# A transformer block on one core: an earlier bound for the third head group, spare banks and matmuls of ones in forced waits, a repeated bias column, and a summed residual in the tail

## The chip, the core and the metric

The kernel runs on one core of a Trainium2 chip. The metric is the device time of one execution in microseconds, lower is better; times are medians of several executions. Before the change the three runs shown took 1149.47, 1150.96 and 1151.28 us, so the median is 1150.96 us. The profile was taken of one further execution of 1149.56 us.

## What is computed

One pre-norm transformer block for 2048 rows of width 1024, in bfloat16, with 32 heads of width 32 and a hidden width of 3584:

```python
def _A_ref(x, wqkv, wo):                      # softmax attention, 32 heads
    qkv = (x @ wqkv) -> q, k, v per head
    p = softmax(q @ k.T * Dh ** -0.5)
    return (p @ v) @ wo
def _B_ref(x, w1, b1, w2, b2):
    return gelu_tanh(x @ w1 + b1) @ w2 + b2

h  = x + _A_ref(_layernorm(x), wqkv, wo)
h2 = h + _B_ref(_layernorm(h), w1, b1, w2, b2)
```

## The kernel before, in words

The kernel is written out by a small planner in Python. Every instruction is recorded as a task with what it reads and writes and with an assumed cost; the planner keeps a clock for each engine, decides from these clocks which instruction comes next on TensorE (PE), and so fixes one order for each engine. The chip then runs each engine's list in that order, with semaphores for the dependences. An assumed cost therefore changes the order, not only a number.

**The exponentials.** Softmax is done in 512 units (`u`, numbered from 0). A unit is one block of queries of 256 rows, one group `g` of four heads and 256 keys. The scores of a unit (`qk`, L1130) fill four PSUM banks (two pairs); ScalarE (ACT) then makes two exponentials of 128x1024 elements (L1139), one for each pair. Units use three pairs of banks, 0/1, 2/3 and 4/5, in turn, two pairs for each unit. Bank 6 (`OD`) gathers the products with the values and the sums (`pv`, L1215); bank 7 alone is left for everything else. Eight units of one head group and one query half make an item; `finish_item` (L1226 to L1230) divides at its end on VectorE (DVE). There are 64 items; each head group of the first 512 queries takes two, so that group 2 (the third) begins at unit 32 and group 5 (the sixth) at unit 80.

**The bound.** An exponential needs a bias, so that it cannot overflow. The bias of a group is made from the largest norm of its keys and of its queries: `sumsq` (four matmuls at L632 and a maximum, L635), then `spread` (a diagonal L643, one matmul L529, a maximum L646), then four small DVE instructions in `bias_of` (L675 to L681). The first exponential of a new group cannot start before.

**Fill.** Between scores and value products the planner places other matmuls, called fill here: a generator yields them one after the other. `fill0` makes the keys (`proj_k`), queries (`proj_q`) and values (`proj_v`) that are not there yet, group by group, with the steps of the bounds (`knorm_a`, `knorm_b`, `qnorm_a`, `qnorm_b`) put beside a named group; then come the feed-forward parts (`ffn`) of each block of 512 rows. A fill group of eight matmuls of 512 columns goes to bank 7 and is read out by DVE (`evac`) before the next can open the bank. A matmul is issued as four matmuls on four quarters of the array side by side (`wide`, L529); four such count as one step in what follows.

**Forced waits.** `qk_prereq` runs ahead of the scores of a unit. Where a mark (a bound, a query block, a flag) is missing, `until` issues fill until it is there. Everything so issued stands on PE ahead of the scores.

**Feed-forward.** In `ffn` the sums with `w1` are read out with the bias and halved in one instruction (`tensor_scalar`, L1538), the rest of the gelu are three DVE instructions and one tanh on ACT (L1550 to L1553) for each pair of column blocks. `rows_out` multiplies with `w2`, adds `b2` (L1448), then the residual (L1451), and stores.

**The tail.** The last block of 512 rows has no exponentials beside it. Its first 256 rows get part of the `w1` product ahead of the end of the exponentials (`early_slices`, slices of 16 steps); the rest runs in `tail` with the gelu on ACT, and `rows_out` at the end, eight times 256 rows by 256 columns.

Of the kernel before, what the change touches and what calls it, by code (L numbers as in the profile page):

```python
# [7 lines left out]
dt = mybir.dt  # L8
# [227 lines left out]
def build_kernel(nc, A_x, A_wqkv, A_wo, B_w1, B_b1, B_w2, B_b2, out):  # L236
# [706 lines left out]
    def fill0():  # L943
        for gen in v_left:
            yield from gen
        load_wkey(2, 0)
        load_wkey(3, 1)

        def key(g, last):
            for tc in range(NCH):  # L950
                if tc == 0 and last is not None:
                    yield from mix(proj_k(g, tc), knorm_a(last))
                elif tc == 1 and last is not None:
                    yield from mix(proj_k(g, tc), knorm_b(last))
                else:
                    yield from proj_k(g, tc)

        yield from key(1, None)
        load_wkey(4, 2)
        load_wqry(4, 3)  # L960
        yield from key(2, 1)
        load_wqry(5, 4)
        load_wqry(6, 5)
        load_wqry(7, 0)
        for tt in range(0, NT, 2):
            yield from proj_v(tt, 1)
        load_wv(1)
        yield from key(3, 2)
        load_wkey(5, 1)
        yield from key(4, 3)  # L970
        load_wkey(6, 2)
        for g in range(4, 8):
            if g < 6:
                yield from mix(proj_q(g, 0), (knorm_a, knorm_b)[g - 4](4))
            else:
                yield from proj_q(g, 0)
        for tt in range(0, NT, 2):
            if tt < 4:
                yield from mix(proj_v(tt, 2), (qnorm_a, qnorm_b)[tt // 2](1, 0))
            else:  # L980
                yield from proj_v(tt, 2)
        yield from key(5, None)
        load_wkey(7, 1)
        yield from key(6, 5)
        for tt in range(0, NT, 2):
            if tt < 4:
                yield from mix(proj_v(tt, 3), (knorm_a, knorm_b)[tt // 2](6))
            else:
                yield from proj_v(tt, 3)
        load_wqry(0, 2)  # L990
        yield from key(7, None)
        load_wqry(1, 1)
        side = deque([knorm_a(7), knorm_b(7)])
        for gq in (1, 0):
            for g in range(gq * 4, gq * 4 + 4):
                if gq == 1 and g in (5, 6):
                    load_wqry(g - 3, g - 2)
                if side:
                    yield from mix(proj_q(g, 1), side.popleft())
                else:  # L1000
                    yield from proj_q(g, 1)
            side = deque([qnorm_a(gq, 1), qnorm_b(gq, 1)])
        while side:
            yield from side.popleft()


    LAST = len(CH) - 1
# [40 lines left out]
        return True  # L1048

    def until(mark, lax=False):  # L1050
        while mark not in marks:
# [27 lines left out]
    def key_of(ci, g):  # L1079
        return ci if ci else NCH + g  # L1080

    def qk_prereq(u):
        ci, g, hf = items[u // NJ]
# [345 lines left out]
    def rows_out(ci, q, t, w2_, gT, B_g, g_ch, ost, B_ost, hch, B_hch, b2s, coming=None):  # L1429
# [6 lines left out]
        for lo_fc, hi_fc, u in ((0, cut, 0), (0, cut, 1), (cut, FC, 0), (cut, FC, 1)):  # L1436
            lo = (t + u) * P
            for fc in range(lo_fc, hi_fc):
                if fc % 8 == 0 and coming:
                    coming.popleft()()  # L1440
                if fc % 2 == 0:
                    yield Need(B_g(fc) + B_g(fc + 1) + [B_w2_[fc // 2]], [B_ps[bank]] if u == 0 and fc == 0 else [],
                               [g_ch[fc + 1]] if fc + 1 in g_ch else [])
                wide(bank, u * 256, 256, gT[:, fc, lo:lo + P], w2[:, fc, :], fc == 0, fc == FC - 1,
                     B_g(fc) + [B_w2_[fc // 2]], [B_ps[bank]] if fc in (0, FC - 1) else [], fc == FC - 1, quad)
        o = (q * 2 + t // 2) % len(B_ost)
        b2_, B_b2_ = b2s
        dve(lambda v: v.tensor_tensor(ost[:, o, :, :], ps[:, bank, :].rearrange("p (u c) -> p u c", u=2),  # L1448
                                      b2_[:, q * 256:(q + 1) * 256].unsqueeze(1).to_broadcast([P, 2, 256]), ALU.add),
            reads=[B_ps[bank]] + B_b2_, writes=[B_ost[o]], cost=690)  # L1450
        add = (E.DVE, lambda v: v.tensor_tensor(ost[:, o, :, :], ost[:, o, :, :], hch[:, t:t + 2, q * 256:(q + 1) * 256], ALU.add),  # L1451
               [B_ost[o]] + [B_hch[2 * (t + u) + q // 2] for u in range(2)], [B_ost[o]], 430)
        r0 = CH[ci][0] + t * P

        def store():
            dma(out2[r0:r0 + 2 * P, q * 256:(q + 1) * 256].rearrange("(u p) c -> p u c", p=P), ost[:, o, :, :], 131072,
                reads=[B_ost[o]], lanes=lanes_o, is_out=True)
            if ci < NCH - 2 and q % 2:
                for u in range(2):
                    load_rows(r0 + 512 + u * P, t + u, q // 2)  # L1460
        stores.append(chain([add, ("call", store, [B_ost[o]], [], 0)]))

    def ffn(ci):
# [62 lines left out]
        for bk in range(FC // 2):  # L1526
            s = w1s[bk]
            for u in range(2):
# [6 lines left out]
                    w2s[0][2].popleft()()  # L1535

                def evac(bank, fc=fc):
                    dve(lambda v: v.tensor_scalar(gT[:, fc, 0:w], ps[:, bank, 0:w], b1f[:, fc:fc + 1], 0.5, ALU.add, ALU.mult),  # L1538
                        reads=[B_ps[bank], Bf_b1f], writes=[B_gT[fc]], cost=100 + 1.2 * w)
                    if fc % 2 == 0:  # L1540
                        return
                    gs = gelu_i[0] % NG
# [69 lines left out]
    def early_slices():  # L1612
# [7 lines left out]
        while early["n"] < FC // 2 - AHEAD and not early["stop"]:  # L1620
# [14 lines left out]
                         [B_ps[bank]] if dc in (0, DC - 1) else [], dc == DC - 1, quad)  # L1635
            for u in range(2):
                fc = 2 * bk + u
                dve(lambda v, fc=fc, u=u: v.tensor_scalar(gT[:, fc, 0:256], ps[:, bank, u * 256:u * 256 + 256], b1f[:, fc:fc + 1], None, ALU.add),
                    reads=[B_ps[bank], Bf_b1f], writes=[B_gT[2 * fc]], cost=420)
        while coming:  # L1640
            coming.popleft()()
# [1 line left out]
    def tail():  # L1643
# [83 lines left out]
            load_more()  # L1727
        while rest:
            rest.popleft()()
        b2s = load_b2(LAST, v_off + 28672)  # L1730
        ost, B_ost = sb("ost_t", [P, 8, 2, 256], dt.bfloat16, nbufs(8), at=f["x3_off"])
        hch, B_hch = last["hch"]
        for q in range(4):
            for t in (0, 2):
                yield from rows_out(LAST, q, t, w2s[q], gT, lambda fc: [B_gT[2 * fc + t // 2]], {}, ost, B_ost, hch, B_hch, b2s)
            if q < 2:
                w2s.append(load_w2(LAST, q + 2, v_off + q * 14336, True))

# [12 lines left out]
    while u < NU or pending:  # L1751
# [63 lines left out]
        elif q_r <= t + 90:  # L1815
            burst()
        else:
            best = min(q_r, p_r if p_r + TURN + step <= due else INF, f_r if f_r + TURN + step <= due else INF)
            if best == INF:
# [131 lines left out]
```

## Time and profile before

| what | value |
|---|---|
| median of three runs | 1150.96 us |
| profiled execution | 1149.56 us, span 1147.8 us |
| PE busy | 1086.5 us (95%) |
| ACT busy | 1042.0 us (91%) |
| DVE busy | 683.3 us (60%) |
| first exponential begins | 52.26 us |
| mean granted PE clock | 0.996 of full |

The span runs from the first instruction to the last; 1.8 us of the execution lie around it. Busy shares are means over stages with different limits, and so it is the idle time of the engine that bounds a stage, and who ended it, that is to be read.

### The profile page before, as it was taken

To read this page: it belongs to the slowest core of one execution; us is meant where nothing else is said; L and a number is where in the kernel's file an instruction comes from. 1 tells how busy PE (TensorE), PEld (TensorE's weight loads), DVE (VectorE), ACT (ScalarE), POOL (GpSimd) and SP (SyncE) were. 2 spreads that over 40 slices of the span, in tenths; PEclk is the share of its full clock that TensorE was granted. 3 is DMA by queue.
4 is the path that set the end of the run, shared out by engine and by line. 5 is a ranking of instruction groups with operands and counts; after the bars stand their busy time and mean duration, and the time that the engine had idled before them with its cause. 6 is when DMAs were issued, how large, how long until landed. Compare 5 with 4: busy or idle time off the path is not lost.

```text
span 1147.8 us, 54608 instructions
## 1 busy us (share of the span) xinstructions
PE 1086.5 (95%) x25370; PEld 658.6 (57%) x25370; DVE 683.3 (60%) x1219; ACT 1042.0 (91%) x1158; POOL 21.2 (2%) x59
## 2 busy tenths in 40 slices
PE   6999999899998999999999999999999999999998
PEld 3646456464444445767444446675544476676887
DVE  8564565555666778545567787545678755556011
ACT  7798999899999999999999999999999999996410
POOL 2100000000000000000000000000000000000000
PEclk9999999999999999999999999999999999999999
DMA  9201000003341244342613343321223332426923
GB/s 264 58 21 40 15 9 3 21 4 103 67 85 58 76 117 115 92 122 60 135 30 95 90 126 99 96 82 31 77 77 109 107 110 72 83 81 187 246 79 87
DMA packets 197941, 98.43 MB, mean 86 GB/s; under 512 B 53328, under 2 KB 194640, under 8 KB 197712
## 3 DMA queue, kind: packets, MB, share of 16 engines
q1 hardware_dynamic: 197712, 94.93, 30.9%
q8 instruction: 198, 3.24, 1.2%
q14 instruction: 31, 0.25, 0.1%
HBM read 88.09 MB, written 4.19 MB: 80 GB/s over the span
## 4 chain that ended last, share of the span: by engine, by line
ACT 50%; PE 33%; issue 10%; DVE 6%; DMA 0%; POOL 0%; ACTq 0%; DVEq 0%; POOLq 0%
ACT PT L1139 47%; PE ps L529 13%; PE ps L524 8%; PE ps L1215 5%; PE ps L1130 4%; ACT tm L1552 3%; DVE lnst L481 1%; PE ps L803 1%; DVE Rg L1228 1%; DVE Rg L1226 1%; DVE QT L1230 1%; PE ps L858 1%; DVE rcp L1227 0%; DVE gT L1538 0%; DVE gT L1553 0%
## 5 line engine op out<-in xcount | busy, mean ns | idle before, releaser
L1139 ACT ACTIVATE PT<-ps 128x1024 bf16<-128x1024 f32 x1024 | 952.0, 1145 | 13.4 <-DVE biasm L681 9.7
L1164 DVE TENSOR_TENSOR FS<-PT 128x1024 bf16<-128x1024 bf16 x252 | 172.2, 688 | 146.7 <-ACT PT L1139 119.0
L1215 PE MATMUL ps<-PT,V 128*32 128x256 bf16 x4096 | 224.9, 274 | 11.6 <-ACT PT L1139 6.1
L1130 PE MATMUL ps<-QT,KT 32*128 32x256 bf16 x4096 | 203.9, 273 | 18.1 <-ACT PT L1139 14.5
L529 PE MATMUL ps<-hnT,w 128*32 128x512 bf16 x2688 | 172.6, 381 | 6.1 <-DVE gT L1538 4.5
L529 PE MATMUL ps<-w,gT 128*32 128x256 bf16 x5376 | 172.6, 273 | 0.7 <-issue 0.6
L1130 PEld LDWEIGHTS ps<-QT,KT 32*128 32x128 bf16 x4096 | 61.1, 92 | 168.0 <-ACT PT L1139 157.7
L529 PEld LDWEIGHTS ps<-w,gT 128*32 128x32 bf16 x5376 | 141.1, 97 | 10.5 <-issue 5.6
L1215 PEld LDWEIGHTS ps<-PT,V 128*32 128x32 bf16 x4096 | 106.0, 96 | 62.0 <-ACT PT L1139 16.2
L1215 PE MATMUL ps<-PT,ones 128*32 128x256 bf16 x2080 | 132.3, 274 | 0.0
L529 PEld LDWEIGHTS ps<-hnT,w 128*32 128x32 bf16 x2688 | 61.5, 96 | 75.5 <-issue 28.4
L1538 DVE TENSOR_SCALAR gT<-ps,b1f 128x512 bf16<-128x512 f32 x84 | 63.0, 750 | 46.0 <-PE ps L529 44.4
L1215 PE MATMUL ps<-FS,ones 128*32 128x256 bf16 x1008 | 72.4, 277 | 0.0
L1215 PEld LDWEIGHTS ps<-PT,ones 128*32 128x32 bf16 x2080 | 56.4, 97 | 10.1
L529 PE MATMUL ps<-xnTe,wk 128*32 128x512 bf16 x832 | 56.6, 395 | 4.3 <-DVE kmax L646 2.3
L1553 DVE SCALAR_TENSOR_TENSOR gT<-tm,gT 128x1024 bf16<-128x1024 bf16 x42 | 51.1, 1219 | 1.4 <-ACT tm L1552 1.0
L1551 DVE SCALAR_TENSOR_TENSOR tm<-tm,gT 128x1024 bf16<-128x1024 bf16 x42 | 51.3, 1222 | 0.9
L1552 ACT ACTIVATE tm<-tm 128x1024 bf16<-128x1024 bf16 x42 | 50.1, 1193 | 0.0
L524 PE MATMUL ps<-w,gT_t 128*128 128x256 bf16 x448 | 49.1, 273 | 0.0
L1448 DVE TENSOR_TENSOR ost_t<-ps,b 128x512 bf16<-128x512 f32 x8 | 5.5, 692 | 72.6 <-PE ps L524 72.6
L524 PEld LDWEIGHTS ps<-w,gT_t 128*128 128x128 bf16 x448 | 43.8, 98 | 5.1
L1678 ACT ACTIVATE gT_t<-ps,b1f 128x256 bf16<-128x256 f32 (+1 forms) x36 | 17.2, 518 | 28.5 <-PE ps L524 28.5
(140 smaller groups left out, 931.4 us busy)
## 6 DMA issues: line engine op xcount, KB each, us to landing
w<-in_B_w_dram SPq DMA_DIRECT2D x42, 512.0 KB, 3.8
w<-in_B_w_dram SPq DMA_DIRECT2D x168, 128.0 KB, 3.6
w_t<-in_B_w_dram SPq DMA_DIRECT2D x12, 512.0 KB, 6.7
xr<-in_A_x_dram SPq DMA_DIRECT2D x16, 256.0 KB, 6.9
wk<-in_A_wqkv_dram SPq DMA_DIRECT2D x16, 256.0 KB, 3.2
wq<-in_A_wqkv_dram SPq DMA_DIRECT2D x16, 256.0 KB, 4.7
w_e<-in_B_w_dram SPq DMA_DIRECT2D x32, 128.0 KB, 2.4
w<-in_B_w_dram SPq DMA_DIRECT2D x14, 256.0 KB, 5.5
```

Source lines behind the costliest of these rows:

```text
L481: steps.append((E.DVE, lambda v, c=c: v.bn_stats(lnst[:, s, i, c * 6:(c + 1) * 6], x_ap[:, c * 512:(c + 1) * 512]), [B_x], [B], 690))
L524: pe(lambda p: p.matmul(ps[:, bank, lo:lo + n], lhsT, rhs, start=start, stop=stop), reads=reads, writes=writes, inc=inc, cost=mm(n))
L529: pe(lambda p, r=r: p.matmul(ps[32 * r:32 * r + 32, bank, lo:lo + n], lhsT[:, 32 * r:32 * r + 32], rhs, start=start, stop=stop, tile_posit ...
L1130: pe(lambda p, k=k, kt=kt, r=r, b=b: p.matmul(ps[:, b, k * 256:(k + 1) * 256], KT[32 * r:32 * r + 32, g, kt * P:(kt + 1) * P], QT[32 * r:3 ...
L1139: act(lambda a, safe, i=i, b=b: a.activation(PT[:, o_, 2 * i:2 * i + 2, :], ps[:, b:b + 2, :], ACT.Exp, bias=0.0 if safe else biasm[:, g, ...
L1164: dve(lambda v: v.tensor_tensor(FS[:, f_, :, :], PT[:, o_, :, 0:256], PT[:, o_, :, 256:512], ALU.add), reads=B_PT[o_], writes=[B_FS[f_]], ...
L1215: pe(lambda p, d=d, r=r, lhsT=lhsT, rhs=rhs, n=n: p.matmul(ps[32 * r:32 * r + 32, OD, d * 256:(d + 1) * 256], lhsT, rhs, start=(start and ...
L1538: dve(lambda v: v.tensor_scalar(gT[:, fc, 0:w], ps[:, bank, 0:w], b1f[:, fc:fc + 1], 0.5, ALU.add, ALU.mult), reads=[B_ps[bank], Bf_b1f], ...
L1551: (E.DVE, lambda v: v.scalar_tensor_tensor(t_, t_, GB, x_, ALU.add, ALU.mult), [Bt] + Bx, [Bt], 1220),
L1552: (E.Activation, lambda a: a.activation(t_, t_, ACT.Tanh, scale=GK), [Bt], [Bt], 946),
L1553: (E.DVE, lambda v: v.scalar_tensor_tensor(x_, t_, 1.0, x_, ALU.add, ALU.mult), [Bt] + Bx, Bx, 1220)])
L1678: act(lambda a: a.activation(gT[:, fc, lo:lo + n], ps[:, bank, o:o + n], ACT.Gelu_apprx_tanh, bias=b1f[:, fc:fc + 1], scale=1.0), reads=[B ...
```

## The change

1. `fill0` lists its groups first and puts side steps ahead of a group by number. The steps of the third group's bound, before beside the first two groups of the next keys, now stand ahead of the last of eight value groups. The other side steps keep their places.
2. A forced wait in `qk_prereq` lets fill use two more banks, the pair that the coming unit doesn't take.
3. In a forced wait, and where the planner sees PE and ACT both idle, matmuls of ones are issued into the coming unit's first bank, as long as the planner's idle time is over 330 ns.
4. The read-out of the `w1` sums adds a repeated column of `b1` with `tensor_tensor`; the halving of the gelu is left out there, its constants follow, and it is done in `rows_out` (by 0.5) for all but the last block. The planner's cost of a read-out is 690 instead of 714.
5. In the tail, residual and `b2` are summed once into an f32 tile `hb` (four DVE instructions); `rows_out` then needs one addition for each store. The last 256 rows by 256 columns are done as two parts of 128 rows with a store each.

```diff
-    GC = 8.0 * 0.044715
-    GB = 2.0 / GC
+    GC = 0.044715
+    GB = 1.0 / GC
...
+        keys(2)
+        loads(asked(load_wqry, 5, 4), asked(load_wqry, 6, 5), asked(load_wqry, 7, 0))
+        beside(7, 7, knorm_a(2), knorm_b(2))
+        vals(1)
+        loads(asked(load_wv, 1))
+        keys(3)
...
     def until(mark, lax=False):
+        if lax and mark not in marks and at_u[0] is not None:
+            k = 2 * ((2 * at_u[0] + 2) % 3)
+            fbanks.items = [7, k, k + 1]
+            fbanks.i = 0
+            until_(mark, lax)
+            fbanks.items = [7]
+        else:
+            until_(mark, lax)
...
+            if lax:
+                awake(fill_ready())
             if not do_fill():
                 raise RuntimeError(f"never made: {mark}")
+
+    def awake(t):
+        b = qk_banks(u)[0]
+        while t < INF and max(plan.free[E.PE], plan.ready(E.PE, [], [B_ps[b]])) + 330 < t:
+            for r in range(4):
+                pe(lambda p, r=r: p.matmul(ps[32 * r:32 * r + 32, b, :], ones_pp[:, 0:32], ones_pp[:].unsqueeze(1).to_broadcast([P, 4, P]),
+                                           start=True, stop=True, tile_position=(0, 32 * r), skip_group_check=True),
+                   reads=[B_ones], writes=[B_ps[b]] if r in (0, 3) else [], inc=r == 3, cost=mm(512) if r == 0 else 1, kind="C")
...
+        if ci == LAST:
+            hb, B_hb = b2s
+            if lone is not None:
+                r0, t, o = r0 + lone * P, t + lone, (o + lone) % len(B_ost)
+                dve(lambda v: v.tensor_tensor(ost[:, o, lone, :], ps[:, bank, lone * 256:lone * 256 + 256], hb[:, t, q * 256:(q + 1) * 256], ALU.add),
+                    reads=[B_ps[bank], B_hb[t]], writes=[B_ost[o]], cost=430)
+                dma(out2[r0:r0 + P, q * 256:(q + 1) * 256], ost[:, o, lone, :], 65536, reads=[B_ost[o]], lanes=lanes_o, is_out=True)
+                return
...
-        dve(lambda v: v.tensor_tensor(ost[:, o, :, :], ps[:, bank, :].rearrange("p (u c) -> p u c", u=2),
-                                      b2_[:, q * 256:(q + 1) * 256].unsqueeze(1).to_broadcast([P, 2, 256]), ALU.add),
+        dve(lambda v: v.scalar_tensor_tensor(ost[:, o, :, :], ps[:, bank, :].rearrange("p (u c) -> p u c", u=2), 0.5 if ci < LAST else 1.0,
+                                             b2_[:, q * 256:(q + 1) * 256].unsqueeze(1).to_broadcast([P, 2, 256]), ALU.mult, ALU.add),
             reads=[B_ps[bank]] + B_b2_, writes=[B_ost[o]], cost=690)
...
-                    dve(lambda v: v.tensor_scalar(gT[:, fc, 0:w], ps[:, bank, 0:w], b1f[:, fc:fc + 1], 0.5, ALU.add, ALU.mult),
-                        reads=[B_ps[bank], Bf_b1f], writes=[B_gT[fc]], cost=100 + 1.2 * w)
+                    dve(lambda v: v.tensor_tensor(gT[:, fc, 0:w], ps[:, bank, 0:w], b1f[:, fc:fc + 1].to_broadcast([P, w]), ALU.add),
+                        reads=[B_ps[bank], Bf_b1f], writes=[B_gT[fc]], cost=690)
...
+        hb, B_hb = b2s = sb("hb", [P, 4, D], dt.float32, nbufs(4), at=xl_off)
+        for t4 in range(4):
+            dve(lambda v, t4=t4: v.tensor_tensor(hb[:, t4, :], hch[:, t4, :], b2_[:], ALU.add),
+                reads=B_hch[2 * t4:2 * t4 + 2] + B_b2_, writes=[B_hb[t4]], cost=1220)
```

More of the change, by code (lines that the diff above doesn't have):

```diff
@@ L947, in fill0 @@
         load_wkey(3, 1)
[L949 to L1002, printed above, removed]
@@ L1003, in fill0, with keys, vals, queries @@
-        while side:
-            yield from side.popleft()
+        groups, sides = [], {}
+        def keys(g):
+            groups.extend(proj_k(g, tc) for tc in range(NCH))
+        def vals(q):
+            groups.extend(proj_v(tt, q) for tt in range(0, NT, 2))
+        def queries(lo, hi, tc):
+            groups.extend(proj_q(g, tc) for g in range(lo, hi))
+        def beside(a, b, ga, gb):
+            sides.setdefault(len(groups) + a, []).append(ga)
+            sides.setdefault(len(groups) + b, []).append(gb)
@@ new lines, in fill0 @@
+        keys(3)
+        loads(asked(load_wkey, 5, 1))
+        beside(0, 1, knorm_a(3), knorm_b(3))
+        keys(4)
+        loads(asked(load_wkey, 6, 2))
+        beside(0, 1, knorm_a(4), knorm_b(4))
+        queries(4, 8, 0)
+        beside(0, 1, qnorm_a(1, 0), qnorm_b(1, 0))
+        vals(2)
+        keys(5)
+        loads(asked(load_wkey, 7, 1))
+        beside(0, 1, knorm_a(5), knorm_b(5))
+        keys(6)
+        beside(0, 1, knorm_a(6), knorm_b(6))
+        vals(3)
+        loads(asked(load_wqry, 0, 2))
@@ new lines, in fill0 @@
+        keys(7)
+        loads(asked(load_wqry, 1, 1))
+        beside(0, 1, knorm_a(7), knorm_b(7))
+        queries(4, 5, 1)
+        loads(asked(load_wqry, 2, 3))
+        queries(5, 6, 1)
+        loads(asked(load_wqry, 3, 4))
+        queries(6, 8, 1)
+        beside(0, 1, qnorm_a(1, 1), qnorm_b(1, 1))
+        queries(0, 4, 1)
+        beside(0, 1, qnorm_a(0, 1), qnorm_b(0, 1))
+        for i, gen in enumerate(groups):
+            for side in sides.pop(i, ()):
+                yield from side
+            yield from gen
@@ L1007, in build_kernel @@
+        for i in sorted(sides):
+            for side in sides[i]:
+                yield from side
     LAST = len(CH) - 1
@@ L1441, in rows_out @@
                 if fc % 2 == 0:
[L1442 removed]
+                    yield Need(B_g(fc) + B_g(fc + 1) + [B_w2_[fc // 2]], [B_ps[bank]] if u == (lone or 0) and fc == 0 else [],
                                [g_ch[fc + 1]] if fc + 1 in g_ch else [])
```

33 lines of the change are left out of this document (27 added, 6 removed).

## Prediction

> **What bounds the kernel now.** I read the busy times on the page, then the waits of ACT, then ACT's timeline where it waits, then the stretches.
>
> ```profile
> PE 1086.5 (95%) x25370; PEld 658.6 (57%) x25370; DVE 683.3 (60%) x1219; ACT 1042.0 (91%) x1158; POOL 21.2 (2%) x59
> ```
> ```profile
> ACT gT_t L1678 <- PE ps L524: 28.5, 19, 8.9
> ACT PT L1139 <- DVE biasm L681: 9.7, 2, 4.8
> ACT PT L1139 <- PE ps L1130: 2.8, 4, 1.2
> ```
> ```profile
> 300.00:1046.30 746.30, 717.33 (x18424) 419.06 (x18416) 488.57 (x803) 744.88 (x811) 9.62 (x21) 1.00 0.34 90
> 1046.30:1144.30 98.00, 96.87 (x881) 82.61 (x880) 18.26 (x35) 21.44 (x41) 1.14 (x3) 1.00 0.57 153
> 1144.30:1147.80 3.50, 0.00 (x0) 0.00 (x0) 1.12 (x2) 0.00 (x0) 0.00 (x0) 1.00 0.13 37
> ```
>
> The stretches list, after their length, the busy time of PE, weight loads, DVE, ACT and POOL, then PE's clock. The highest busy share is PE's, but it doesn't set the pace everywhere. From 300 to 1046 us ACT works 744.88 of 746.30 us, while PE has 29 us to spare: the exponentials set the time. From 1046.3 to 1144.3 it is PE (96.87 of 98.00); then come 3.5 us for the last output. So a gain is worth something in three places only: where ACT waits between exponentials (9.7 + 2.8 us in all), in PE's work after the last exponential, and behind the last matmul. The 28.5 us of L1678 belong to the tail, where PE is the bound.
>
> The waits between exponentials sit in two places (start, length, idle before):
>
> ```profile
> 116.19 1.94 ACT L1139 ACTIVATE PT<-ps 128x1024 bf16<-128x1024 f32 x2 [4.84 <-DVE biasm L681]
> 119.34 2.85 ACT L1139 ACTIVATE PT<-ps 128x1024 bf16<-128x1024 f32 x3 [1.21 <-PE ps L1130]
> ```
> ```profile
> 194.84 11.14 ACT L1139 ACTIVATE PT<-ps 128x1024 bf16<-128x1024 f32 x12
> 210.80 1.94 ACT L1139 ACTIVATE PT<-ps 128x1024 bf16<-128x1024 f32 x2 [4.81 <-DVE biasm L681]
> 213.21 7.54 ACT L1139 ACTIVATE PT<-ps 128x1024 bf16<-128x1024 f32 x8 [0.48 <-PE ps L1130]
> ```
>
> They are the starts of the third group (unit 32) and the sixth (unit 80): 4.84 + 1.21 and 4.81 + 0.48, together **11.34 us**. The rest of the 2.8 us is two waits of 0.56 us far apart, which I leave as they are.
>
> **Part 1, the third group's bound.** The instruction orders of the two programs can be compared without a time. In the new one group 2's norm matmuls stand behind the scores of unit 29 and its diagonal behind those of unit 30, and ACT reads the flag ahead of unit 31's exponentials; the bias is some 1.5 units ahead of its use, and the 4.84 + 1.21 us go. What is late next is the sixth group. Its bound keeps its place in the list of fill, but the old wait at unit 32 had pushed PE's fill ahead; now ACT reaches unit 80 with less fill done. In the old order 8 steps of keys stand between the scores of units 79 and 80, in the new one 18, and ten steps of ones.
>
> What the new wait costs is worked out along the order, with durations of the old wait:
>
> ```profile
> 203.29 0.40 PE L1130 MATMUL ps<-QT,KT 32*128 32x256 bf16 x8 [0.22 <-ACT PT L1139]
> 204.90 1.91 PE L529 MATMUL ps<-xnTe,wk 128*32 128x512 bf16 x32 [0.89 <-DVE kn L635]
> 206.63 0.29 PE L1215 MATMUL ps<-PT,V 128*32 128x256 bf16 x4
> 206.74 0.30 PE L1215 MATMUL ps<-PT,ones 128*32 128x256 bf16 x4
> ...
> 208.23 0.24 PE L529 MATMUL ps<-dg,ones_pp 128*32 128x128 bf16 x4 [0.55 <-DVE dg L643]
> 208.40 0.40 PE L1130 MATMUL ps<-QT,KT 32*128 32x256 bf16 x8
> ```
> ```profile
> 204.07 0.69 DVE L635 TENSOR_REDUCE kn<-ps 128x1 f32<-128x512 f32 x1 [0.56 <-PE ps L632]
> 206.86 0.69 DVE L582 CAST KT<-ps 128x512 bf16<-128x512 f32 x1 [2.10 <-PE ps L529]
> 207.59 0.42 DVE L583 TENSOR_TENSOR sqk<-KT 128x512 bf16<-128x512 bf16 x1
> 207.93 0.25 DVE L643 TENSOR_SCALAR dg<-ident,kn 128x128 bf16<-128x128 bf16 x1
> 208.09 0.44 DVE L1226 STREAM_TRANSPOSE Rg<-ps 128x256 f32<-128x256 f32 x1
> 209.63 0.28 DVE L646 TENSOR_REDUCE kmax<-ps 128x1 f32<-128x128 f32 x1
> ```
>
> - The scores of unit 79 start at 203.29; their row says 0.40 us, the next matmul overlaps a little of it, and I take 0.33. Call 203.62 zero. ACT runs dry at 194.84 + 11.14 = 205.98, that is at 2.36.
> - PE then has 2 steps of keys (32 matmuls took 206.63 - 204.90 = 1.73, so 0.22 a step: 0.43), 9 steps of value products (0.11 each: 1.0), then 8 steps of keys whose read-out starts 206.86 - 204.90 = 1.96 after their begin: 3.4.
> - DVE has in its new order: read-out (0.73 to the next start) and square (0.34), the four instructions that finish an item (209.63 - 208.09 = 1.54), the maximum of norms (0.72), one more read-out and square (1.07), the diagonal (0.25 and 0.05 to its matmul), 0.29 more to the next maximum (the diagonal's matmul of 0.24 and a handover of 0.05), and from there to the exponential 210.80 - 209.63 = 1.17. Sum 6.15.
> - So ACT starts at 3.4 + 6.15 = 9.55, and waits 9.55 - 2.36 = **7.2 us** instead of 4.81.
>
> **Part 2, the spare banks.** The two banks lent to fill at unit 80 are 0 and 1, which are among the four that unit 81 takes for its scores. A fill group opened in one of them must be finished and read out first. In the new order 13 steps of keys stand between the scores of units 80 and 81; the first 8 end a borrowed bank's group. Its read-out ends 0.33 + 1.96 + 0.69 = 2.98 us after the scores of unit 80 start, the exponential can follow some 0.55 us behind that (a handover of 0.1 and 119.34 - 118.89 = 0.45 from scores to exponential), and unit 80's exponentials end 1.3 + 1.94 = 3.24 after those scores start (1.17 + 0.29 - 0.17 from scores to exponential, 208.40 - 208.23 = 0.17 being how far they stand behind the diagonal's matmul): a wait of **0.3 us**, between nothing and the 1.21 us of the old first wait.
>
> ```profile
> 118.89 0.40 PE L1130 MATMUL ps<-QT,KT 32*128 32x256 bf16 x8
> ```
>
> One place is new: between the scores of units 116 and 117 PE's order has a value product that reads unit 116's own exponentials. In the old order that stands only at the two forced waits, in the new only here and at unit 80. There the scores of 117 wait until ACT is done: handover about 0.25, two steps of 0.11, 0.45 to the exponential: **0.9 us**.
>
> New waits: 7.2 + 0.3 + 0.9 = 8.4 us against 11.34: a gain of **2.9 us**.
>
> **Part 3, matmuls of ones.** They are ten steps of 512 columns (2.2 us), all between units 79 and 80 and placed where PE waits for DVE's square and diagonal, so they cost nothing unless they end later than DVE: at worst a few 0.22 us. What they could hold off shows here:
>
> ```profile
> 111.88:115.29 3.41, 1.34 (x36) 0.61 (x28) 2.90 (x8) 0.00 (x0) 0.00 (x0) 1.00 0.05 16
> 115.29:118.71 3.42, 3.35 (x32) 1.13 (x32) 0.63 (x5) 1.94 (x2) 0.00 (x0) 0.52 0.02 5
> 207.46:210.87 3.41, 1.70 (x43) 0.70 (x36) 2.94 (x12) 0.07 (x1) 0.00 (x0) 1.00 0.00 0
> 210.87:214.28 3.41, 3.41 (x44) 1.12 (x40) 1.12 (x2) 2.93 (x4) 0.00 (x0) 0.52 0.01 2
> ```
>
> After 3.41 us in which PE was busy 1.34 and 1.70 us, the clock is at half for the next 3.41 us. That made the 1.21 and 0.48 us behind the old waits; in the new wait PE is filled almost throughout, so I put no half clock there. The Trainium skill (TensorE: Matmul & The Clock Gate, "Why this matters for your kernels") asks only that no idle gap exceeds about 3 us; by that neither old wait would have lost its clock, and the ones would be worth nothing. The rows above speak against it: the longest single gap in them was 1.16 us.
>
> **Part 4, repeated column and planner costs.** The form (f32 from PSUM plus a repeated f32 column) isn't in the trace. Nearest:
>
> ```profile
> L1538 DVE TENSOR_SCALAR gT<-ps,b1f 128x512 bf16<-128x512 f32 x84 | 63.0, 750 | 46.0 <-PE ps L529 44.4
> L1448 DVE TENSOR_TENSOR ost_t<-ps,b 128x512 bf16<-128x512 f32 x8 | 5.5, 692 | 72.6 <-PE ps L524 72.6
> L1551 DVE SCALAR_TENSOR_TENSOR tm<-tm,gT 128x1024 bf16<-128x1024 bf16 x42 | 51.3, 1222 | 0.9
> ```
>
> I take L1448's 692 ns (same size, two tensors), at worst 1222. 84 x 58 ns = 4.9 us less DVE work, under a stage that ACT bounds with 744.88 of 746.30: nothing. The halving in `rows_out` is one more operand on 24 instructions of 0.69 us, nothing either.
>
> **Part 5, the tail.** From the last exponential PE has four projections, what is left of an early slice, and the tail's steps. In the new order the left part is 64 matmuls instead of 16, the tail's own `w1` steps are 336 instead of 352.
>
> ```profile
> 1095.20 49.07 PE L524 MATMUL ps<-w,gT_t 128*128 128x256 bf16 x448
> 1101.52 0.69 DVE L1448 TENSOR_TENSOR ost_t<-ps,b 128x512 bf16<-128x512 f32 x1 [37.82 <-PE ps L524]
> 1144.31 0.69 DVE L1448 TENSOR_TENSOR ost_t<-ps,b 128x512 bf16<-128x512 f32 x1 [4.96 <-PE ps L524]
> 1145.04 0.42 DVE L1451 TENSOR_TENSOR ost_t<-ost_t,hch_t 128x512 bf16<-128x512 bf16 x1
> 1145.49 0.37 SPq L290 DMA_DIRECT2D out_dram<-ost_t  x1
> ```
> ```profile
> L1230 DVE TENSOR_TENSOR QT<-ps,Rg 128x256 bf16<-128x256 f32 x64 | 27.2, 424 | 2.2
> ```
> ```profile
> 1082.86 0.67 SPq L289 DMA_DIRECT2D b<-in_B_b_dram  x1
> ...
> 1107.62 1.26 SPq L290 DMA_DIRECT2D w<-in_B_w_dram  x2
> ```
>
> A step is 49.07 / 448 = 0.109 us: 12 more and 16 fewer, **0.4 us** gained. The four sums into `hb` cost 4 x 1.22 = 4.9 us at most and lie in the 37.82 us in which DVE waits for the first output; they need `b2`, whose load is asked for at 1082.86, 18.7 us ahead of it. Without that cover the first read-out alone would be late, and PE has other banks meanwhile. At the end the store was issued 1145.49 - 1144.31 = 1.18 us after the read-out began. Now one addition of 128x256 stands there; that size with two f32 inputs takes 424 ns (L1230), so 1.18 - 0.45 = **0.7 us** is gained. The store halves; I give that nothing. On SP's queue the loads of the third and fourth `w2` parts now stand behind one more store each, about 1 us; the third part, asked for at 1107.62, is needed half way through the 49.07 us, at 1119.7.
>
> **Sum.** 1149.56 - 2.9 - 0.4 - 0.7 = 1145.6 for the profiled execution. That execution is 1.4 us under the median of 1150.96; for the median 1150.96 - 4.0 = **1147.0 us**.
>
> **Rivals.**
> 1. *The time is given back in full at the sixth group.* The same fill must be done before its bound, so the waits might again add up to 11 us (half clock in spite of the ones, one window at half pace costing 1.7 us, and 1.2 us each at units 81 and 117). For it: PE was busy 95%, and the order does move 10 steps there. Against it: the chain above. Only the tail's 1.1 us would remain: 1149.8.
> 2. *The read-out of `w1` sums is slow* with the repeated column, at L1551's 1222 ns instead of 750. The fill there has one bank, so PE waits each time: 84 x 0.47 = 40 us against PE's 29 us to spare from 300 to 1046; it decides from about 0.35 us more on each. It would give 1147 + 11 = 1158, slower. Against it: L1448, same size, 692.
> 3. *The bound isn't earlier in effect*, because something else holds unit 32 back. The waits stay as before: 1149.8.
>
> **How the numbers follow.** Forecast 0.64, rival 1 0.22, rival 2 0.08, rival 3 0.06. About 0.2% (2.3 us) is what a measurement of this kernel can tell from no change, so faster begins under 1148.7. The forecast's own range is 1144.5 to 1149: 1.5 us either way for the waits, 0.5 for the tail, and what medians of three differ. Rivals 1 and 3 lie up to 1150.5; I leave out rival 2. Range 1144.0 to 1150.5. A little of the forecast falls into the same: faster 0.62, same 0.28, slower 0.10.
>
> **What would show it.** ACT should have no wait for the bias near 111 us and one of about 7.2 us near 200; waits of under 1 us behind it and near 270; no half clock at either start; the read-out of `w1` sums at 0.69 us; 1.1 us less between last exponential and end. A wait over 10 us at the sixth group, a read-out over 1.1 us, or new waits beyond 300 us would make the prediction wrong.

## The result and the profile after

The changed kernel takes **1144.88 us** (median of six runs, 1144.68 to 1145.98) against 1150.95 us for the kernel before (six runs, 1149.47 to 1152.45): 6.07 us less, a ratio of 0.995 with an interval of 0.9938 to 0.9963. Forecast were 1147.0 us, 4.0 less. Two further comparisons of the same two kernels, below, gave 4.1 and 4.3 us less; why the first one is larger is part of what follows. The profiled execution took 1145.98 us with a span of 1144.2, that is 3.6 us less than the profiled one of before.

The page's first part, and what ACT waited for (us in total, times, longest; the row of L1726 belongs to the tail, the other two lie between the exponentials):

```profile
PE 1086.8 (95%) x25445; PEld 655.4 (57%) x25450; DVE 681.5 (60%) x1220; ACT 1041.2 (91%) x1159; POOL 21.8 (2%) x59
```
```profile
ACT gT_t L1726 <- PE ps L524: 28.3, 18, 10.2
ACT PT L1172 <- DVE biasm L681: 7.4, 1, 7.4
ACT PT L1172 <- PE ps L1163: 2.9, 7, 0.8
```

The busy shares tell nothing: they stand as before. The waits for the bias do: two of 4.8 us have become one of 7.4. Waits for scores (L1163) have grown from four to seven, with about the same sum: 0.25 us at unit 60, which the old kernel doesn't have, 0.47 and 0.84 behind the long wait, and four beyond 300 us with 1.4 in all, where the old kernel had two with 1.1. ACT's timeline (start, length, how many exponentials, idle before) says where they are:

```profile
53.19 110.58 ACT L1172 ACTIVATE PT<-ps 128x1024 bf16<-128x1024 f32 x120 [0.37 <-issue]
164.02 37.16 ACT L1172 ACTIVATE PT<-ps 128x1024 bf16<-128x1024 f32 x40 [0.25 <-PE ps L1163]
208.59 1.94 ACT L1172 ACTIVATE PT<-ps 128x1024 bf16<-128x1024 f32 x2 [7.42 <-DVE biasm L681]
211.00 66.28 ACT L1172 ACTIVATE PT<-ps 128x1024 bf16<-128x1024 f32 x72 [0.47 <-PE ps L1163]
278.11 22.10 ACT L1172 ACTIVATE PT<-ps 128x1024 bf16<-128x1024 f32 x24 [0.84 <-PE ps L1163]
...
1043.82 1.28 ACT L1889 ACT_TABLE_LOAD   x1
```

The first line is the point of part 1: 120 exponentials without a stop, past unit 32, where the old kernel waited 4.84 us. The three longest waits are at units 80, 81 and 117: 7.42 + 0.47 + 0.84 = 8.73 us against 11.34. The table load after the last exponential begins 990.63 us after the first exponential, before it was 1046.32 - 52.26 = 994.06: 3.4 us less. From there to the span's end it is 1144.2 - 1043.82 = 100.4 us against 101.5: 1.1 us less. The first exponential itself begins 0.9 us later, which is no part of the change: its start lay between 52.0 and 53.6 us in the profiles of this study, of unchanged programs too. 3.4 + 1.1 - 0.9 = 3.6.

The stretches (length, then busy time of PE, weight loads, DVE, ACT, POOL, then PE's clock, DMA's busy share and GB/s), for the long wait, the exponentials after 300 us, and the tail:

```profile
200.90:208.60 7.70, 7.70 (x152) 3.76 (x148) 5.34 (x15) 0.28 (x2) 0.00 (x0) 1.00 0.16 36
300.00:1043.80 743.80, 715.91 (x18384) 415.76 (x18378) 483.11 (x804) 742.39 (x809) 9.91 (x21) 1.00 0.33 90
1043.80:1140.70 96.90, 95.51 (x904) 81.78 (x906) 20.39 (x34) 21.43 (x43) 1.14 (x3) 1.00 0.61 159
```

In the wait ACT is idle and PE is busy all of 7.70 us at full clock: it is a wait for PE's and DVE's chain, not an idle chip. PE's timeline there, with the value products and a short run of keys left out, shows with what it was filled (L1088 are the matmuls of ones):

```profile
198.69 0.40 PE L1163 MATMUL ps<-QT,KT 32*128 32x256 bf16 x8
...
200.45 1.90 PE L529 MATMUL ps<-xnTl,wk 128*32 128x512 bf16 x32
...
202.61 0.82 PE L1088 MATMUL ps<-ones_pp 128*32 128x512 bf16 x12
203.26 0.73 PE L632 MATMUL ps<-sqk,blk 128*32 128x512 bf16 x4
203.61 2.11 PE L529 MATMUL ps<-xnTe,wk 128*32 128x512 bf16 x32
205.34 1.89 PE L1088 MATMUL ps<-ones_pp 128*32 128x512 bf16 x28
207.13 0.24 PE L529 MATMUL ps<-dg,ones_pp 128*32 128x128 bf16 x4
207.30 0.40 PE L1163 MATMUL ps<-QT,KT 32*128 32x256 bf16 x8
```

The group of keys at 203.61 stands in another bank than the norms' sums of L632 ahead of it, for DVE reads those only later, which in one bank would have held the keys back:

```profile
205.00 0.68 DVE L635 TENSOR_REDUCE kn<-ps 128x1 f32<-128x512 f32 x1
```

The read-out of the `w1` sums and DVE in the tail:

```profile
L1586 DVE TENSOR_TENSOR gT<-ps,b1f 128x512 bf16<-128x512 f32 x84 | 58.0, 690 | 48.4 <-PE ps L529 47.9
```
```profile
1086.02 4.63 DVE L1783 TENSOR_TENSOR hb<-hch_t,b 128x1024 f32<-128x1024 bf16 x4 [23.51 <-DMA b<-in_B_b_dram]
1098.88 0.69 DVE L1491 TENSOR_TENSOR ost_t<-ps,hb 128x512 bf16<-128x512 f32 x1 [8.23 <-PE ps L524]
...
1141.67 0.42 DVE L1487 TENSOR_TENSOR ost_t<-ps,hb 128x256 bf16<-128x256 f32 x1 [2.63 <-PE ps L524]
```

The read-out has fallen from 750 to 690 ns. The four sums into `hb` lie in idle time, and 8.23 us of it are left behind them.

### The profile page after: what moved, and what is told of

It reads as the page before. It is cut to its first block, busy times and chain, and to the rows that moved or that the text cites. A ratio compares the mean times of both kernels' runs of the same rounds, so it can differ in the third digit from the quotient of the medians.

```text
span 1144.2 us, 54773 instructions
## 1 busy us (share of the span) xinstructions
PE 1086.8 (95%) x25445; PEld 655.4 (57%) x25450; DVE 681.5 (60%) x1220; ACT 1041.2 (91%) x1159; POOL 21.8 (2%) x59
## 4 chain that ended last, share of the span: by engine, by line
ACT 44%; PE 40%; issue 9%; DVE 5%; DMA 1%; SPq 0%; POOL 0%; ACTq 0%; DVEq 0%; POOLq 0%
ACT PT L1172 41%; PE ps L529 18%; PE ps L524 7%; PE ps L1248 7%; PE ps L1163 5%; ACT tm L1600 2%; DVE lnst L481 1%; PE ps L803 1%; DVE Rg L1259 1%; DMA w_t<-in_B_w_dram 1%; DVE Rg L1261 1%; PE ps L858 1%; DVE QT L1263 1%; DVE FS L1197 0%; DVE gT L1586 0%
## 5 line engine op out<-in xcount | busy, mean ns | idle before, releaser
L1163 PE MATMUL ps<-QT,KT 32*128 32x256 bf16 x4096 | 203.7, 273 | 20.8 <-ACT PT L1172 15.7
L1163 PEld LDWEIGHTS ps<-QT,KT 32*128 32x128 bf16 x4096 | 60.8, 92 | 172.8 <-ACT PT L1172 160.4
L1586 DVE TENSOR_TENSOR gT<-ps,b1f 128x512 bf16<-128x512 f32 x84 | 58.0, 690 | 48.4 <-PE ps L529 47.9
L1726 ACT ACTIVATE gT_t<-ps,b1f 128x256 bf16<-128x256 f32 (+1 forms) x36 | 16.7, 506 | 28.3 <-PE ps L524 28.3
L1248 PEld LDWEIGHTS ps<-FS,ones 128*32 128x32 bf16 x1016 | 26.7, 95 | 23.5 <-issue 19.2
```

The source lines that it names most:

```text
L1163: pe(lambda p, k=k, kt=kt, r=r, b=b: p.matmul(ps[:, b, k * 256:(k + 1) * 256], KT[32 * r:32 * r + 32, g, kt * P:(kt + 1) * P], QT[32 * r:3 ...
L1248: pe(lambda p, d=d, r=r, lhsT=lhsT, rhs=rhs, n=n: p.matmul(ps[32 * r:32 * r + 32, OD, d * 256:(d + 1) * 256], lhsT, rhs, start=(start and ...
L1586: dve(lambda v: v.tensor_tensor(gT[:, fc, 0:w], ps[:, bank, 0:w], b1f[:, fc:fc + 1].to_broadcast([P, w]), ALU.add), reads=[B_ps[bank], Bf_ ...
L1726: act(lambda a: a.activation(gT[:, fc, lo:lo + n], ps[:, bank, o:o + n], ACT.Gelu_apprx_tanh, bias=b1f[:, fc:fc + 1], scale=1.0), reads=[B ...
```

## The experiments

Two things had to be explained: why the time fell by more than 4.0 us, and which part of the change did it. **Theory A**: what comes on top is half clock. The old kernel loses PE's clock behind its waits, in some executions more than its profile shows, and the changed kernel doesn't, since matmuls of ones and lent banks keep PE busy. The rivals are other places: the bound's move, the read-out or the tail are worth more than the sum gave them. The expectations call the first A; the letters after it stand for such other places. The experiments ran in three groups, each beside the kernel before, which took 1149.57 us beside e1 to e4, 1149.22 beside e5 to e8 and 1149.65 beside e9 to e12. "Full clock" means a mean granted clock of 1.000 over the execution.

**e1, the kernel before once more**, with no edit.

> The kernel before, unchanged, for a second profile. The measured gain of 6.1 us is 2.1 us more than the chain of waits and the tail give (4.0). Theory A: the spells of half clock, which begin in aligned stretches of 3.41 us after a stretch in which PE was busy about half of the time or less, fall differently in each execution; in the profile of before they fell cheaply (1.21 and 0.48 us behind the two waits). Then this profile shows the same two waits for the bias of 4.8 us, but another sum of the waits for the scores, up to 2 us more, and times that spread over about 3 us. Theory B: the rest of the gain comes from the many later stretches (read-out, order of the work). Then the waits between exponentials sum to 12.5 us here as in the first profile, and what is left is a longer time from 300 us on.

1149.70 us, ratio 1.0007 (0.9999 to 1.0016). Its profile fell on an execution of 1148.5 us without any half clock. ACT's waits there, then the stretches that answer to the four that the prediction shows (same work, 0.93 us later behind the first wait, 0.40 earlier behind the second):

```profile
117.12 88.47 ACT L1139 ACTIVATE PT<-ps 128x1024 bf16<-128x1024 f32 x96 [4.83 <-DVE biasm L681]
210.40 90.42 ACT L1139 ACTIVATE PT<-ps 128x1024 bf16<-128x1024 f32 x98 [4.81 <-DVE biasm L681]
```
```profile
112.81:116.22 3.41, 1.34 (x36) 0.61 (x28) 2.89 (x8) 0.00 (x0) 0.00 (x0) 1.00 0.06 20
116.22:119.64 3.42, 2.84 (x56) 1.30 (x60) 1.75 (x7) 2.52 (x3) 0.00 (x0) 1.00 0.02 5
207.06:210.47 3.41, 1.71 (x43) 0.69 (x36) 2.94 (x12) 0.07 (x1) 0.00 (x0) 1.00 0.00 0
210.47:213.88 3.41, 2.90 (x60) 1.09 (x56) 1.12 (x2) 3.41 (x4) 0.00 (x0) 1.00 0.01 2
```

PE is as idle as before (busy 1.34 and 1.71 us of 3.41), yet the next stretch has clock 1.00, and the 1.21 and 0.48 us behind the old waits are gone. So half clock is a matter of the single execution, and those 1.69 us are its price at the two waits, as theory A says. Over 83 executions of the old kernel (e1 and those beside the three groups) the time goes with the mean granted clock: 1147.88 us on average at 1.000 (8 of them), 1149.07 at 0.999 (26), 1149.50 at 0.998 (11), 1150.28 at 0.997 (17), 1151.15 at 0.996 (16); over all, 1149.73. The order isn't strict: the five below 0.996 averaged 1150.3, and the eight at 1.000 lay between 1146.2 and 1148.9. If those eight stand for the kernel without half clock, it costs 1.85 us on average, and 3.3 at a clock of 0.996.

**e2, the changed kernel without ones.**

```diff
     def awake(t):
+        return
```

> The changed kernel without the matmuls of ones; the order of all other instructions is the same. Theory A: PE idles 0.65 and 1.5 us inside the long wait at unit 80, a spell of half clock follows in part of the executions, and the steps of keys behind it take up to 1.7 us longer: median 1145.4 to 1146.5 and a wider spread than the changed kernel's 1.3 us. Theory B, and the rule that only an idle gap of about 3 us costs the clock: no spell, median 1144.9 as with the ones.

1145.15 us, ratio 0.9964 (0.9951 to 0.9977), and full clock in all six runs: no slower. The wait, and the stretch in which it lies:

```profile
208.57 1.94 ACT L1173 ACTIVATE PT<-ps 128x1024 bf16<-128x1024 f32 x2 [7.42 <-DVE biasm L681]
```
```profile
200.90:208.60 7.70, 5.68 (x112) 2.67 (x108) 5.34 (x15) 0.28 (x2) 0.00 (x0) 1.00 0.16 36
```

Without the ones PE is busy 5.68 of 7.70 us, and the clock holds all the same. Theory A expected 1145.4 to 1146.5 us and a wider spread, which was too much: in the changed kernel the ones cost nothing and bring nothing that can be told.

**e3, the changed kernel with one bank for fill.**

```diff
-            fbanks.items = [7, k, k + 1]
+            fbanks.items = [7]
```

> The changed kernel with bank 7 alone in forced waits, ones kept. The same 18 steps of keys stand between units 79 and 80, but each group waits for the read-out of the one before it. Theory A: the wait for the bias grows from 7.4 to about 9.2 us (one read-out and its handovers, 1.2, and the norm matmuls behind a read-out, 0.6), the waits at units 81 and 117 (0.47 and 0.84) go, since their orders are not there: about 1145.5. A rival, that the borrowed banks don't matter because DVE's chain sets the wait: 7.4 us and 1144.

1146.74 us, ratio 0.9973 (0.9964 to 0.9983), 1.6 us more than e2 beside it.

```profile
210.18 90.42 ACT L1172 ACTIVATE PT<-ps 128x1024 bf16<-128x1024 f32 x98 [9.45 <-DVE biasm L681]
```

The wait is 9.45 us, and the 0.47 and 0.84 us behind it are gone with the lent banks. 9.45 - 8.73 = 0.7 us is seen in the waits. The planner also made six early slices here instead of seven, and the profile takes 0.4 us longer than e2's from table load to end (100.5 against 100.1). The remaining 0.5 us was not traced; 1145.5 was expected. All twelve runs had full clock: with the ones, a single bank keeps it too.

**e4, the kernel before with the bound's move alone.**

```diff
+            if tt == NT - 2:
+                yield from knorm_a(2)
+                yield from knorm_b(2)
...
-        yield from key(3, 2)
+        yield from key(3, None)
```

> The kernel before with the third group's bound moved and nothing else. Theory A: the first pair of waits (4.84 + 1.21) goes, the one at unit 80 grows to about 9.2 us with one bank, plus 1 to 2 us of half clock behind it without ones: waits of 10 to 11 us against 11.3, so 1149.5 to 1150.5, hardly a gain: the move alone is given back at the sixth group. If the move by itself is what gains, the wait stays near 7.4 and the time is 1147.

1149.19 us, ratio 1.0000 (0.9989 to 1.0011): the move alone gains nothing in the median. ACT and PE:

```profile
209.43 91.34 ACT L1142 ACTIVATE PT<-ps 128x1024 bf16<-128x1024 f32 x99 [9.45 <-DVE biasm L681]
```
```profile
204.63 1.91 PE L529 MATMUL ps<-xnTe,wk 128*32 128x512 bf16 x32 [1.83 <-DVE kn L635]
207.96 0.24 PE L529 MATMUL ps<-dg,ones_pp 128*32 128x128 bf16 x4 [1.42 <-DVE dg L643]
```

The two waits of 4.8 have become one of 9.45: given back. With a single bank PE stands idle for 1.83 us, until DVE has read the norms' sums (kn), and 1.42 us more, and the executions spread from 1146.70 to 1151.83 us: five at clock 0.998 or less took 1149.1 and more, the three at 1.000 took 1146.7 to 1147.2.

**e5, the kernel before with the ones alone** (the function `awake` and its two calls).

> The kernel before with the matmuls of ones alone: five steps of them ahead of unit 32, four ahead of unit 80, no other order changed. In the first runs on this question the kernel before took 1147.8 us where its mean granted clock was 1.000 and 1150.6 where it was 0.996 or 0.997. Theory A (the part of the gain that the prediction lacked is half clock, which comes and goes between executions): granted clock 1.000 in nearly all executions, waits for the bias as before (4.8 and 4.8 us), median 1147 to 1148, 2 us under the kernel before, spread under 2 us. Theory B (ones are worth nothing, the gain comes from the order): as the kernel before, 1149.5 to 1151.

1147.70 us, ratio 0.9986 (0.9977 to 0.9994), with waits of 4.84 and 4.81 us as in the old kernel. The clock was at least 0.998 in all twelve runs. At an unchanged wait, 1.5 us came from nothing but PE being kept busy: theory A, where it says that the old waits lose clock. The least busy 3.41 us at the two waits now have 2.13 us of PE work, before 1.27 and 1.70. But only five of the twelve had full clock, where nearly all were expected, and the profiled one, at 0.999, shows why: from 819.10 us PE was busy 1.80 us of 3.41, where no bound is awaited and no ones are placed, and from 822.51 to 825.92 the clock was 0.51. The old kernel loses clock at this third place too (rows in the last section). In the profiles of the changed kernel and of e2 no stretch of 3.41 us between the exponentials has less than 1.96 us of PE work, so the third place went without the ones. Which part of the change did that wasn't tested.

**e6, the changed kernel once more**, with no edit.

> The changed kernel again, beside the others on one chip: 1144.9, granted clock 1.000 in all executions. Theory A also wants the difference to an execution of before at full clock to be about 3 us, theory B 6.

1145.15 us, ratio 0.9969 (0.9957 to 0.9981): 4.1 us less than before, not 6.1.

**e7, a value product less early at unit 117.** The planner's choice between two kinds of value products was mended for one branch of its loop, so that none reading unit 116's own exponentials stands ahead of the scores of 117.

```diff
-    def pv():
-        e = sums.popleft() if due_sum() or (sums and plan.ready(E.PE, pv_reads(sums[0]), []) <= plan.free[E.PE] + 150) else pending.popleft()
+    def pv(early=False):
+        s_r = plan.ready(E.PE, pv_reads(sums[0]), []) if sums else INF
+        if early and sums and pending and s_r <= plan.ready(E.PE, pv_reads(pending[0]), []):
+            s_r = 0.0
+        e = sums.popleft() if due_sum() or (sums and s_r <= plan.free[E.PE] + 150) else pending.popleft()
...
```

> The changed kernel with the planner's slip at unit 116 mended: where it chose to place a value product because the sums of a folded unit would be ready first, it then placed another product that waits for the unit's own exponentials. The wait of 0.84 us at unit 117 should go and nothing else change up to there: 0.8 us less than the changed kernel on the same chip, about 1144.1. If the wait comes back later, because PE's fill is what limits the first 128 units, the time is the changed kernel's.

1142.99 us, ratio 0.9949 (0.9938 to 0.9961): 2.2 us less than e6 beside it, where 0.84 were at stake. It is told further at e11.

**e8, the changed kernel with the old tail**: no `hb`, no last parts of 128 rows.

```diff
...
-            for t, lone in (((0, None), (2, None)) if q < 3 else ((0, None), (2, 0), (2, 1))):
+            for t, lone in ((0, None), (2, None)):
```

> The changed kernel with the tail's output as before: addition of b2, then of the residual, 256 rows at the last. By the chain of the last output 0.7 us more than the changed kernel; the time from the last exponential to the end 101.1 instead of 100.4. A rival, that the smaller last store also lands sooner: 1.0 us or more.

1146.19 us, ratio 0.9975 (0.9965 to 0.9984): 1.0 us more than e6. From table load to the span's end it took 101.3 us, in e6 100.0; 0.95 of that lies behind the last matmul (3.46 against 2.51 us). The prediction had 0.7 for this.

**e9, the old read-out of the `w1` sums**, with the planner's cost and so the order kept; the constants of the gelu and the addition of `b2` go back with it.

```diff
-                    dve(lambda v: v.tensor_tensor(gT[:, fc, 0:w], ps[:, bank, 0:w], b1f[:, fc:fc + 1].to_broadcast([P, w]), ALU.add),
+                    dve(lambda v: v.tensor_scalar(gT[:, fc, 0:w], ps[:, bank, 0:w], b1f[:, fc:fc + 1], 0.5, ALU.add, ALU.mult),
...
```

> The changed kernel with the read-out of the w1 sums, the constants of the gelu and the addition of b2 as before, with the planner's cost of the changed kernel, so that the order of all instructions stays. The read-out's mean goes from 690 to 750 ns, 84 x 60 ns = 5 us more work on DVE. By the prediction (ACT bounds that stage) the time is the changed kernel's, 1144.9 to 1145.2. If the stage were bound by the read-outs in the one bank, 1147 or more.

```profile
L1586 DVE TENSOR_SCALAR gT<-ps,b1f 128x512 bf16<-128x512 f32 x84 | 63.0, 750 | 46.8 <-PE ps L529 46.0
```

1145.63 us, ratio 0.9967 (0.9951 to 0.9982), beside 1145.38 for e12: 5 us more DVE work change nothing that can be told. DVE waits 46.0 us for these sums here and 47.9 in the changed kernel's first profile.

**e10, a shorter way to the sixth bound.** On top of e7, its norms of keys are laid side by side with the group ahead, and the end of an item is put behind the bound in forced waits.

```diff
-        beside(0, 1, knorm_a(5), knorm_b(5))
+        beside(0, 0, knorm_a(5), knorm_b(5))
...
```

> The mended kernel with the two steps of the sixth group's bound side by side (no group of keys between them) and, in a forced wait, the end of the item behind the bound's instructions. By the chain the wait for the bias at unit 80 falls from 7.4 to about 5.1 us (1.54 of the item's end and 0.8 of the second read-out leave it). If waits are only moved (8 steps of keys are then still to do): a new wait for the bias at unit 112, and the mended kernel's time of 1143 or up to 1 us more. If the chain alone counts: 1140.8.

1146.21 us, ratio 0.9970 (0.9958 to 0.9983), slower than e11 beside it by 2.6 us.

```profile
206.80 58.91 ACT L1179 ACTIVATE PT<-ps 128x1024 bf16<-128x1024 f32 x64 [5.36 <-DVE biasm L681]
269.34 1.94 ACT L1179 ACTIVATE PT<-ps 128x1024 bf16<-128x1024 f32 x2 [3.63 <-DVE biasm L681]
271.85 28.55 ACT L1179 ACTIVATE PT<-ps 128x1024 bf16<-128x1024 f32 x31 [0.58 <-PE ps L1170]
```

The wait at unit 80 fell as hoped, from 7.42 to 5.36 us. But the next bound but one, at unit 112, now makes ACT wait 3.63 + 0.58 us where it had not waited: 9.57 us in all against 7.88 in e11. The wait was moved, and grew. The place was expected, but the time was not: up to 1 us more than e7's 1143 at worst. 1.7 of the 2.6 us are in these waits. Part of the rest is clock: five of the twelve runs were below full clock, and the seven at full clock averaged 1145.8 us, 2.0 more than e11.

**e11, the mended kernel once more**, and **e12, the changed kernel a third time**, with no new edits.

> The mended kernel again, beside the changed one on the same chip: it took 2.2 us less, though only a wait of 0.84 us is gone in its trace, with a start 0.9 us earlier. If the rest was chance, 0.8 to 1.2 us less than the changed kernel here; if the order behind unit 116 gains more, 2 us again.

> The changed kernel for comparison on the same chip: 1144.9 to 1145.2, granted clock 1.000, waits 7.42, 0.47 and 0.84 us.

e11 took 1143.65 us, ratio 0.9948 (0.9934 to 0.9962), e12 1145.38 us, ratio 0.9963 (0.9949 to 0.9976): the mended kernel is ahead by 1.7 us, by 2.2 in the pair before. It is the best version found, ahead of both kernels. ACT's waits in e11, to be set beside those of the changed kernel above:

```profile
ACT PT L1172 <- DVE biasm L681: 7.4, 1, 7.4
ACT PT L1172 <- PE ps L1163: 0.7, 2, 0.5
```

Two waits for scores instead of seven: with the 0.84 us at unit 117 the small ones beyond 300 us have gone as well (1.4 us in four in the changed kernel's first profile, 0.6 in e12's). From first exponential to table load it took 987.82 us against 989.73 in e12, 1.9 less, of which the waits show 2.1 - 0.7 = 1.4. Why the small waits went with the edit, and the other 0.5 us, stays open.

## Why the prediction was right, point by point

- **Part 1 held.** No wait at unit 32; a wait of 7.42 us at unit 80 where 7.2 were worked out. The chain itself was right to 0.02 us: from the scores of unit 79 (198.69 + 0.33) to the exponential (208.59) it took 9.57 us, the sum said 9.55, and no term of it was off by more than 0.05. ACT ran dry 0.2 us sooner than assumed.
- **Part 2 held.** 0.47 us at unit 81 for 0.3, and 0.84 at unit 117 for 0.9. The 0.25 us at unit 60 were not foreseen. New waits beyond 300 us, which were to speak against the prediction, did come, but they are small: four of 1.4 us in all against two of 1.1 before, and 0.3 and 0.6 us in the profiles of e6 and e12. The lent bank's read-out ends at 210.28 and the scores follow at 210.55; I had given that handover 0.1 us instead of 0.27.

```profile
209.59 0.69 DVE L582 CAST KT<-ps 128x512 bf16<-128x512 f32 x1 [1.12 <-PE ps L529]
```
```profile
210.55 0.40 PE L1163 MATMUL ps<-QT,KT 32*128 32x256 bf16 x8
```

- **Part 3 was right in what it cost, and half right in what it did.** Ten steps of ones (12 + 28 matmuls) stand where they were expected and cost nothing, and half clock did not come back in the new wait. But I put that to PE being filled by the ones, and e2 shows that here the lent banks alone do it. The ones alone do it too (e3), and in the old kernel they are worth 1.5 us by themselves (e5).
- **Part 4 held**: 690 ns for 692, and nothing in the time (e9).
- **Part 5 held in its sum, but not term by term.** The tail is 1.1 us shorter in this profile, as summed (0.4 + 0.7). But from table load to the first `w2` matmul it is only 0.14 us shorter (1092.56 - 1043.82 = 48.74 against 48.88), and from the end of the last matmul to the span's end 0.96 (2.57 against 3.53). The 0.4 is there in e6 and e12 (48.45, 0.43 less); in the first profile the 240 `w1` matmuls ahead of `w2` took 26.65 us instead of 26.36, and the chain that ended last runs there through the load of `w_t`. The 0.7 was too small: the store is issued about 0.4 us after the read-out begins, as summed, but the span then ends 2.1 us after that issue instead of 2.3, and the prediction gave the halved store nothing. So it is partly luck that the sum fits here; in e6 and e12 the tail is 1.4 us shorter. The old end costs 1.0 us (e8).
- **The sum.** For the profiled execution it gave 1145.6 us; the changed kernel's came to 1145.98. Where it went too far up is the step after it: "That execution is 1.4 us under the median of 1150.96; for the median 1150.96 - 4.0". That carries the old kernel's spread over to the new one, and most of it is gone: 83 executions of the old kernel lay between 1146.16 and 1152.98 us, 19 of the changed one between 1143.98 and 1146.43, with a clock of 1.000 in 16 and 0.999 in three. But it wasn't its clock that made the profiled execution a quick one: at 0.996 it lay 1.6 us under the average of that clock. Its first exponential began 0.9 us earlier than in e1; the rest stays open.

So the gain has three terms. At full clock the old kernel averaged 1147.88 us and the changed one 1145.11, a difference of 2.8: the tail 1.1 (1.4 in e6 and e12), the waits 9.64 - 8.73 = 0.9, and 0.5 to 0.8 that no one place in the profiles explains. Half clock gives the rest, 1.85 us in the old kernel on average against about 0.1 in the new. The forecast's 4.0 has the same terms: 1.69 of half clock (1.21 + 0.48), 9.65 - 8.4 = 1.25 for the waits, and 1.1 for the tail. The six old runs of the first comparison had a median 1.2 us above the average of all 83; that is the larger part of what sets its 6.07 above the 4.1 and 4.3 of e6 and e12, which the forecast of 4.0 meets.

**The rivals.** The first, that the time is given back in full at the sixth group, is refuted for the whole change, but it is just what the bound's move does alone (e4: one wait of 9.45 us, half clock, ratio 1.0000), and in e10 a wait was moved to a later group once more. Two things decided between it and the forecast. In the wait it was the lent banks: with them PE's fill goes on while DVE reads out, and the wait is 7.42 instead of 9.45. In the time the clock counts as much: e3 has the wait of 9.45 but full clock (and the new end), and took 1146.74 against 1149.57 beside it. The slow read-out (690 ns instead of 1222) and the bound without effect (no wait at unit 32) are refuted by their rows.

## What to carry to other kernels

A wait removed early in a stage comes back at the next deadline if the work that it had let another engine do is still owed; ask what that engine is short of (here a bank to put sums in) before moving the deadline. A forecast is made for one profiled execution; ask first what makes the executions of the old kernel differ, and whether the change takes that away, before it is carried over to a median. And look at the mean granted clock of every run, not of one profile: the same program with the same idle time kept full clock in one execution and lost it in the next.

## What the runs showed of the hardware

- Spells of half clock in the old kernel's first profile last 3.41 us, and each follows a stretch of 3.41 us in which PE was busy about half the time or less: 1.34 and 1.70 us (the prediction's rows), and 1.78 us at the third place, where no bound is awaited:

```profile
821.99:825.40 3.41, 1.78 (x48) 0.71 (x44) 1.91 (x6) 3.41 (x5) 1.14 (x3) 1.00 0.91 274
825.40:828.81 3.41, 3.41 (x100) 2.50 (x96) 1.38 (x3) 2.85 (x4) 0.00 (x0) 0.50 0.42 120
```

- The same idle stretches kept full clock in e1, so something that isn't in the program has a part in it. No limit is shown either: e10, whose profile has no stretch of 3.41 us between the exponentials with less than 1.96 us of PE work, lost clock in five of its twelve runs. The Trainium skill (TensorE: Matmul & The Clock Gate, "Why this matters for your kernels") says that one window of idle halves the clock and that gaps over about 3 us are to be avoided. The length of the spells fits a window of 3.41 us; the limit on gaps doesn't, as the longest gap in the prediction's two stretches was 1.16 us (rows of the kernel before, below). That the window's start falls differently against the program in each execution would explain e1, but that wasn't measured.

```profile
115.36 3.60 PE L529 MATMUL ps<-xnTe,wk 128*32 128x512 bf16 x32 [1.16 <-DVE kmax L646]
209.96 2.65 PE L529 MATMUL ps<-xnTe,wk 128*32 128x512 bf16 x32 [1.16 <-DVE kmax L646]
```
- Reading 128x512 f32 sums out of PSUM took 690 ns with a repeated f32 column as second tensor and 750 ns with the same column as a scalar per row and a second scalar operation (e9).
